# Output layer of an attention and gated-linear kernel: casts one tile ahead, subtractions moved from behind each pass's last product, an earlier split at the change of layers, one zero product instead of three

## The chip, the cores and the metric

One core of one Trainium2 chip. The metric is the device time of one execution in microseconds, as the median of several runs.

## The reference

Sigmoid attention over 8 batches and 12 heads (448 positions, head size 64), then a gated linear layer on the 3584 x 768 result, in fp32:

```python
scores = scale * np.matmul(q, k.transpose(0, 1, 3, 2)) - np.log(S)
attn = 1.0 / (1.0 + np.exp(-scores))
x = np.matmul(attn, v)            # heads side by side: (3584, 768)
gate = 1.0 / (1.0 + np.exp(-(x @ w_gate)))   # w_gate, w_val: 768 x 1536
val = x @ w_val
out = gate * val @ w_out                     # w_out: 1536 x 768
```

`w_gate`, `w_val` and `w_out` arrive as 64-bit floats and are brought to fp32 on the chip.

## The kernel before, in words

The work has three stages on TensorE, one behind the other: attention, the gate and value layer (GLU), and the output layer. Batches are taken in four pairs (`NPAIR`). The two linear layers use a Strassen-like scheme: each 2 x 2 block product is made of seven products (`NP`), so that a stage runs over seven combined operand tiles (index `i`) for each pair. Each operand is split into a high part, rounded to fp32r by a cast, and a low part, the difference. `product` (L316) makes three matmuls for each block: low weight by high operand, high weight by low operand, high by high.

For each operand tile there are therefore two steps before TensorE can use it: the cast on ScalarE (`high`, L164) and the subtraction on VectorE (`low`, L167). Both work on a tile of 128 x 1344. The source comes from DRAM by a load on SP's queue: `load_x` (L157) for the GLU, `load_h` (L337) for the output layer. The next load takes the buffer of a source that was subtracted, and SP waits for that.

All instructions are written in the program's order; each engine runs its own in that order. `tick()` is called after each group and runs what is due by then: stores, weight loads, and the casts and subtractions of weight tiles (`fetch_w`, L359: cast ten ticks after the load, L354, and subtraction twelve ticks after it, L357).

**Attention.** 168 beats (24 head groups by 7 key groups). A beat makes one scores product (L203), one sigmoid on ScalarE (L206) and the values product (L219) of two beats before. Before the first beat three zero products (L272 to L276) run on a zeroed tile. In the last beats the first GLU operands are loaded, x0 is cast and subtracted, and x1 is cast (L303), before the pending values products; x1 is subtracted after them (L308).

**GLU.** Three passes over the weights by four pairs by seven tiles `i` by four products `q` of nine matmuls. Behind a product its reader runs: a copy or sigmoid on ScalarE, an add (L328) or product (L331) on VectorE. Behind the last tile (`i` = 6) the result blocks are combined by subtractions (L420), on GpSimd, in the last half of the last pair on VectorE, and stored as `hs` (L374). The last two tiles (`left` 2 and 1) also prepare the output layer: cast of h0 and h1 at `q` = 1 of the two tiles (L430), subtraction and the next load at `q` = 2 (L434).

**Output layer.** Four pairs by seven passes `i` by three products `o`, each of 18 matmuls: nine with the operand tile h[m], nine with h[m+1]. Here m grows by two for each pass. The readers are copies on ScalarE for `i` = 0 and 1 (L476, L479) and adds on VectorE (L328) for the others. Even tiles have three buffers for the split operand and two for the source, odd tiles two and two (L340, L346). The order behind a product is:

```python
tick()
if o < 2:
    high_h(m + 2 + o)
if o > 0:
    low_h(m + 1 + o)
    load_h(m + 5 + o)
```

So h[m+2] is cast after the first product and subtracted after the second, and h[m+3] is cast after the second product and subtracted after the third, the last one of the pass.

Of the kernel before, what the change touches and what calls it, by code (L numbers as in the profile page):

```python
# [30 lines left out]
def sigmoid_attention_glu_kernel(ctx: ExitStack, tc: tile.TileContext, qk, v, wg, wv, wo, out):  # L31
# [34 lines left out]
    def tick(flush=False):  # L66
        clock[0] += 1
        due = [e for e in later if e[0] <= clock[0] or flush and e[2]]
        later[:] = [e for e in later if e not in due]
        for _, fn, _ in due:  # L70
            fn()
# [97 lines left out]
    def high_x(n):  # L169
        if n < len(x_order):  # L170
            ops[n] = op_tile()
            high(ops[n], x_loaded[n])
# [7 lines left out]
    with tc.manual_schedule(), tc.tile_pool(name="att", bufs=2) as att, tc.tile_pool(name="sc", bufs=2, space=PSUM) as scp, \  # L180
# [88 lines left out]
        units.load()  # L269
        zeros = att.tile([P, 2, S], F32, tag="a", name="a", bufs=3)[:, 0]  # L270
        nc.vector.memset(zeros, 0.0)
        for _ in range(3):  # L272
            sc = scp.tile([P, 2, 512], F32, tag="sc", name="sc")
            for h in range(2):
                for u in range(2):
                    nc.tensor.matmul(sc[halves[u], h, :S], lhsT=zeros[halves[h], :HP], rhs=zeros[halves[h]], start=True, stop=True)  # L276
        beats, beat, done = B * NQ * 7, 0, 0
        for m in range(B * NQ):
            for g in range(7):
                pending.append((m, g, scores(m, g)))  # L280
                if len(pending) > LAG:
                    values(*pending.pop(0))
                if g == 0:
                    load_qk(m + 1)
                if g == LAG:
                    load_v(m + 1)
                if m == 0 and g in (1, LAG):
                    units.load()
                tick()
                beat += 1  # L290
                while done < N_FIRST and done * (beats - 12) < beat * N_FIRST:
                    next(weights)
                    done += 1
                finish_adds()
                if beat == beats - 8:
                    load_x(0)
                    load_x(1)
                if beat == beats - 4:
                    high_x(0)
                if beat == beats - 3:  # L300
                    low_x(0)
                if beat == beats - 1:
                    high_x(1)  # L303
        while pending:
            values(*pending.pop(0))
            finish_adds()
            tick()
        low_x(1)  # L308
        tick(flush=True)

    with tc.manual_schedule(), tc.tile_pool(name="mm", bufs=8, space=PSUM, reuse_waits="tile") as mm:
# [37 lines left out]
        def low_h(m):  # L349
            if m < len(o_order):  # L350
                low(h_ops[m], h_loaded.pop(m))
# [17 lines left out]
        with tc.tile_pool(name="ff", bufs=1, reuse_waits="tile") as ff:  # L369
            def unit(tag, n):  # L370
                return ff.tile([P, S], F32, tag=tag, name=tag, bufs=n)

            def store_h(p, i, j, h):
                nc.sync.dma_start(out=h_src[p][i][j // 3][:, j % 3], in_=h)  # L374

            n = 0
            done, groups, all_groups = 0, 0, 8 * NP * NQUAD
            for s in range(NPASS):
                for p in range(NPAIR):
                    st = [{} for _ in range(NQUAD)]  # L380
                    if s == NPASS - 1 and p == NPAIR - 2:
                        for _ in weights:
                            pass
                    for i in range(NP):
                        for q in range(NQUAD):
                            d, t, jl = st[q], q % 2, q // 2
                            j = s * JS + jl
                            gate = st[q - 1] if t else None
                            if i in (0, 2, 5):
                                d["acc"] = bank()  # L390
                            acc = d["acc"]
                            product(acc, [(W[i][:, q], ops[n], (cols(k), k)) for k in range(HC)], i)
                            if i == 0:
                                d["s1"] = unit("s1", 6)
                                nc.scalar.copy(d["s1"], acc)  # L395
                            elif i == 1:
                                d["11"] = unit("v11" if t else "g11", 4)
                                if t:
                                    mul(d["11"], acc, gate["11"])
                                    after(2, lambda p=p, j=j, h=d["11"]: store_h(p, 0, j, h))  # L400
                                else:
                                    nc.scalar.activation(d["11"], acc, AF.Sigmoid)
                            elif i in (2, 3):
                                k = "u2" if i == 2 else "u3"
                                d[k] = unit(k, 5)
                                add(d[k], acc, d["s1"])
                            else:
                                k, to = {4: ("s1", 1), 5: ("u3", 6), 6: ("u2", None)}[i]
                                add(d[k], acc, d[k])
                                if t:  # L410
                                    mul(d[k], d[k], gate[k])
                                    if to is not None:
                                        after(2, lambda p=p, to=to, j=j, h=d[k]: store_h(p, to, j, h))
                                else:
                                    nc.scalar.activation(d[k], d[k], AF.Sigmoid)  # L415
                                if t and i == 6:
                                    t1, t2, t3, t4 = (unit("t", 7) for _ in range(4))
                                    for o, a, b in ((t1, d["u2"], d["11"]), (t2, d["u3"], t1), (t3, d["u3"], d["u2"]), (t4, d["s1"], t2)):
                                        engine = nc.vector if jl == 1 and s == NPASS - 1 and p == NPAIR - 1 else nc.gpsimd
                                        engine.tensor_tensor(out=o, in0=a, in1=b, op=ALU.subtract)  # L420
                                    for dly, to, h in ((3, 5, t1), (4, 2, t2), (5, 3, t3), (6, 4, t4)):
                                        after(dly + 2 * jl, lambda p=p, to=to, j=j, h=h: store_h(p, to, j, h))
                            tick()
                            left = len(x_order) - n
                            if q == 1:
                                high_x(n + 2)
                                if left in (4, 3):
                                    load_h(4 - left)
                                if left in (2, 1):
                                    high_h(2 - left)  # L430
                            if q == 2:
                                low_x(n + 2)
                                if left in (2, 1):
                                    low_h(2 - left)  # L434
                                    load_h(4 - left)
                            if q == 3:
                                if p == NPAIR - 1:
                                    nextW[i] = new_w(i)
                                    fetch_w(nextW[i], w_src[s + 1][i] if s + 1 < NPASS else o_src[i][:, :NQUAD])
                                if 0 <= 2 * NP - 2 - left < NP:  # L440
                                    fetch_wx(2 * NP - 2 - left)
                            if p < NPAIR - 1 and (s < NPASS - 1 or p < NPAIR - 2):
                                groups += 1
                                while done < N_REST and done * all_groups < groups * N_REST:
                                    next(weights, None)
                                    done += 1
                        ops.pop(n)
                        n += 1
                    if p == NPAIR - 1:
                        old, W[:] = list(W), [nextW[i] for i in range(NP)]  # L450
        with tc.tile_pool(name="fo", bufs=1, reuse_waits="tile") as fo:
# [1 line left out]
                return fo.tile([P, S], F32, tag=tag, name=tag, bufs=3)  # L453

            tick(flush=True)
            for m in range(4, 6):
                load_h(m)
            m = 0
            for p in range(NPAIR):
                st = [{} for _ in range(HC)]  # L460

# [4 lines left out]
                for i in range(NP):  # L466
                    for o in range(HC):
# [25 lines left out]
                                    save(o + mo, b, d[k], queue, a)  # L493
                        tick()
                        if o < 2:
                            high_h(m + 2 + o)
                        if o > 0:
                            low_h(m + 1 + o)
                            load_h(m + 5 + o)
                    h_ops.pop(m)  # L500
                    h_ops.pop(m + 1)
                    m += 2
# [36 lines left out]
```

## Time and profile before

| what | value |
|---|---|
| median of 3 runs | 1207.56 us (1204.35 to 1208.07) |
| profiled execution: its own time | 1207.19 us |
| its span, first to last instruction | 1205.4 us |
| TensorE matmul, busy | 1193.2 us, 99% |
| TensorE weight load, busy | 955.6 us, 79% |
| VectorE, ScalarE, GpSimd, busy | 722.3, 491.5, 321.7 us |
| attention, GLU, output layer (span) | to about 260, to about 883, to the end |

The profile lists instructions by engine: PE is the matmul, PEld the weight load that runs beside it, DVE VectorE, ACT ScalarE, POOL GpSimd, SP the queue that issues the DMAs. A matmul's recorded duration includes its way through the array, so matmuls overlap in the record and a busy PE can still lose time between them. In the timeline the square bracket names the idle time before an instruction and what ended it.

### The profile page before, as it was taken

How to read it: one execution, taken by the hardware profiler on the slowest of the kernel's cores; microseconds unless marked ns; L12 is line 12 of the kernel's file. 1: busy time of each engine (PE TensorE's matmuls, PEld its weight loads, DVE VectorE, ACT ScalarE, POOL GpSimd, SP SyncE). 2: the span in 40 equal slices, each digit the busy share in tenths (PEclk: the TensorE clock that was granted, in tenths of full speed). 3: DMA queues.
4: the chain of work that ended last, by engine and by line, in shares of the span. 5: the costliest groups of instructions: out<-in, count | busy, mean ns of one | idle time of the engine just before them, and what ended most of it. 6: DMA issues, size and time to landing. Idle time of an engine off the chain costs nothing.

```text
span 1205.4 us, 18247 instructions
## 1 busy us (share of the span) xinstructions
PE 1193.2 (99%) x7248; PEld 955.6 (79%) x7248; DVE 722.3 (60%) x827; ACT 491.5 (41%) x553; POOL 321.7 (27%) x244
## 2 busy tenths in 40 slices
PE   9999999999999999999999999999999999999998
PEld 3444444459999999899999999999988898898987
DVE  3344334437888858988876898747675424334333
ACT  6777777762322336232232623224344132132230
POOL 2161524251605315163450516414020000000000
PEclk9999999999999999999999999999999999999999
DMA  7585877877867777776758767466784543544441
GB/s 290 195 291 208 279 230 240 304 234 243 272 224 254 251 250 252 234 277 224 242 195 314 244 231 257 136 227 210 261 286 147 178 168 138 180 141 162 161 144 61
DMA packets 103077, 266.23 MB, mean 221 GB/s; under 512 B 10448, under 2 KB 74192, under 8 KB 102992
## 3 DMA queue, kind: packets, MB, share of 16 engines
q1 hardware_dynamic: 102848, 264.95, 64.1%
q8 instruction: 57, 0.93, 0.3%
q14 instruction: 28, 0.23, 0.1%
q10 hardware_dynamic: 144, 0.11, 0.0%
HBM read 176.95 MB, written 88.08 MB: 220 GB/s over the span
## 4 chain that ended last, share of the span: by engine, by line
PE 72%; DVE 4%; issue 1%; ACT 1%; DVEq 0%
PE acc L322 72%; DVE op L167 3%; DVE w L357 0%; ACT w L354 0%; DVE u L328 0%; ACT op L164 0%; DVE wsum L357 0%; DVE s L328 0%; PE av L219 0%; ACT wsum L354 0%; DVE s L331 0%; DVE u L331 0%; DVEq L534 0%; DVEq L328 0%; ACT u L415 0%
## 5 line engine op out<-in xcount | busy, mean ns | idle before, releaser
L322 PE MATMUL acc<-op,w 128*128 128x448 f32 x4032 | 845.3, 367 | 6.0 <-DVE op L167 4.1
L322 PEld LDWEIGHTS acc<-op,w 128*128 128x128 f32 x4032 | 755.8, 188 | 82.4 <-DVE op L167 12.0
L167 DVE TENSOR_TENSOR op<-src,op 128x1344 fp32r<-128x1344 f32 x140 | 233.3, 1666 | 70.8 <-ACT op L164 70.6
L164 ACT CAST op<-src 128x1344 fp32r<-128x1344 f32 x140 | 183.5, 1316 | 210.7 <-PE acc L322 139.9
L206 ACT ACTIVATE a<-sc,bias 128x896 f32<-128x896 f32 x168 | 169.0, 1007 | 66.5 <-PE sc L203 63.1
L203 PE MATMUL sc<-qk 64*64 64x448 f32 x1344 | 157.0, 538 | 0.4 <-ACT a L206 0.4
L219 PE MATMUL av<-a,v 64*64 64x448 f32 x1344 | 156.4, 536 | 0.7 <-ACT a L206 0.7
L328 DVE TENSOR_TENSOR u<-acc,s 128x448 f32<-128x448 f32 x120 | 74.2, 623 | 103.7 <-PE acc L322 103.3
L328 DVE TENSOR_TENSOR u<-acc,u 128x448 f32<-128x448 f32 (+1 forms) x121 | 73.8, 617 | 68.7 <-PE acc L322 68.6
L203 PEld LDWEIGHTS sc<-qk 64*64 64x64 f32 x1344 | 51.6, 134 | 76.5 <-issue 63.6
L219 PEld LDWEIGHTS av<-a,v 64*64 64x64 f32 x1344 | 51.4, 133 | 75.8 <-issue 74.0
L420 POOL TENSOR_TENSOR t<-u,v 128x448 f32<-128x448 f32 x23 | 37.9, 1648 | 224.9 <-DVE u L331 207.1
L129 POOL TENSOR_TENSOR wsum<-wf 128x384 f32<-128x384 f32 x18 | 20.7, 1153 | 231.7 <-DVE wf L117 231.7
L415 ACT ACTIVATE u<-u 128x448 f32<-128x448 f32 x48 | 27.8, 578 | 119.0 <-DVE u L328 115.0
L415 ACT ACTIVATE s<-s 128x448 f32<-128x448 f32 x24 | 13.9, 579 | 119.2 <-DVE s L328 119.1
L328 DVE TENSOR_TENSOR s<-acc,s 128x448 f32<-128x448 f32 x60 | 37.2, 622 | 40.4 <-PE acc L322 40.4
L322 PE MATMUL acc<-op,wr 128*128 128x448 f32 x216 | 50.7, 371 | 0.0
L245 DVE TENSOR_TENSOR op<-av,op 128x448 f32<-128x448 f32 x24 | 15.0, 623 | 58.9 <-ACT op L236 58.9
L395 ACT COPY s<-acc 128x448 f32<-128x448 f32 x48 | 25.5, 532 | 47.3 <-PE acc L322 41.5
L322 PEld LDWEIGHTS acc<-op,wr 128*128 128x128 f32 x216 | 41.4, 192 | 3.4
L245 DVE TENSOR_TENSOR x<-av,x 128x448 f32<-128x448 f32 x24 | 15.0, 624 | 48.1 <-ACT x L236 48.1
L420 POOL TENSOR_TENSOR t<-u,u 128x448 f32<-128x448 f32 x23 | 43.0, 1868 | 0.0
(51 smaller groups left out, 747.2 us busy)
## 6 DMA issues: line engine op xcount, KB each, us to landing
src<-xs SPq DMA_DIRECT2D x84, 672.0 KB, 4.7
src<-hs SPq DMA_DIRECT2D x56, 672.0 KB, 3.9
hs<-t SPq DMA_DIRECT2D x96, 224.0 KB, 5.2
qk<-qk SPq DMA_DIRECT2D x23, 896.0 KB, 5.0
v<-vv SPq DMA_DIRECT2D x24, 448.0 KB, 4.7
xs<-t SPq DMA_DIRECT2D x48, 224.0 KB, 4.1
w<-ws SPq DMA_DIRECT2D x14, 768.0 KB, 7.2
wr<-wg SPq DMA_DIRECT2D x12, 768.0 KB, 6.4
```

The lines of the kernel that those rows point to most:

```text
L129: nc.gpsimd.tensor_tensor(out=s1, in0=a21, in1=a22, op=ALU.add)
L164: nc.scalar.copy(op[:, 0], src)
L167: nc.vector.tensor_tensor(out=op[:, 1], in0=src, in1=op[:, 0].bitcast(F32), op=ALU.subtract)
L203: nc.tensor.matmul(sc[halves[u], h, :S], lhsT=qkt[halves[h], p, k0:k0 + HP], rhs=qkt[halves[h], p, :S], start=True, stop=True)
L206: nc.scalar.activation(a, sc[:, :, :S], AF.Sigmoid, bias=bias, scale=scale)
L219: nc.tensor.matmul(avs[key][halves[h], :S], lhsT=vt[halves[u], g, h], rhs=a[halves[u], h], start=start, stop=g == last)
L245: nc.vector.tensor_tensor(out=x, in0=other, in1=x, op=ALU.add)
L322: nc.tensor.matmul(acc, lhsT=a, rhs=b, start=first and n == 0, stop=n == len(terms) - 1, skip_group_check=not first)
L328: nc.vector.tensor_tensor(out=o, in0=a, in1=b, op=ALU.add)
L395: nc.scalar.copy(d["s1"], acc)
L415: nc.scalar.activation(d[k], d[k], AF.Sigmoid)
L420: engine.tensor_tensor(out=o, in0=a, in1=b, op=ALU.subtract)
```

## The change

There are four edits. One zero product is made instead of three. The cast of x1 moves behind the pending values products. In the last GLU tile, h1 is cast after group 0 and subtracted after group 1 (before: 1 and 2); h0 stays where it was. In the output layer, h5 is loaded before h4, h2 is cast before the first product, and behind the products the order is: after the first, subtract h[m+2], load h[m+6], cast h[m+3]; after the second, subtract h[m+3], load h[m+7]; after the third, cast h[m+4].

```diff
-        for _ in range(3):
-            sc = scp.tile([P, 2, 512], F32, tag="sc", name="sc")
-            for h in range(2):
-                for u in range(2):
-                    nc.tensor.matmul(sc[halves[u], h, :S], lhsT=zeros[halves[h], :HP], rhs=zeros[halves[h]], start=True, stop=True)
+        sc = scp.tile([P, 2, 512], F32, tag="sc", name="sc")
+        for h in range(2):
+            for u in range(2):
+                nc.tensor.matmul(sc[halves[u], h, :S], lhsT=zeros[halves[h], :HP], rhs=zeros[halves[h]], start=True, stop=True)
...
-                if beat == beats - 1:
-                    high_x(1)
         while pending:
             values(*pending.pop(0))
             finish_adds()
             tick()
+        high_x(1)
         low_x(1)
...
-                                if left in (2, 1):
-                                    high_h(2 - left)
                             if q == 2:
                                 low_x(n + 2)
-                                if left in (2, 1):
-                                    low_h(2 - left)
-                                    load_h(4 - left)
+                            if (left, q) in ((2, 1), (1, 0)):
+                                high_h(2 - left)
+                            if (left, q) in ((2, 2), (1, 1)):
+                                low_h(2 - left)
+                                load_h(4 - left)
...
-            for m in range(4, 6):
+            for m in (5, 4):
                 load_h(m)
             m = 0
+            high_h(2)
...
                         if o < 2:
-                            high_h(m + 2 + o)
-                        if o > 0:
-                            low_h(m + 1 + o)
-                            load_h(m + 5 + o)
+                            low_h(m + 2 + o)
+                            load_h(m + 6 + o)
+                        if o != 1:
+                            high_h(m + 3 + o // 2)
```

## Rows read from the trace of the kernel before

**Rows 1.** The page, busy us, share of the span and instructions of each engine.

```profile
PE 1193.2 (99%) x7248; PEld 955.6 (79%) x7248; DVE 722.3 (60%) x827; ACT 491.5 (41%) x553; POOL 321.7 (27%) x244
```

**Rows 2.** Timeline, output layer, one pass: start, duration, engine, line, tiles.

```profile
1040.77 0.62 DVE L328 TENSOR_TENSOR u<-acc,u 128x448 f32<-128x448 f32 x1 [3.03 <-PE acc L322]
...
1044.42 0.63 DVE L328 TENSOR_TENSOR u<-acc,u 128x448 f32<-128x448 f32 x1 [1.56 <-PE acc L322]
1044.96 1.55 DVE L167 TENSOR_TENSOR op<-src,op 128x1344 fp32r<-128x1344 f32 x1
...
1046.56 0.30 PEld L322 LDWEIGHTS acc<-op,w 128*128 128x128 f32 x2 [0.53 <-DVE op L167]
```

**Rows 3.** Waits of PEld, 895 to 1205: us in total, times, longest.

```profile
PEld acc L322 <- DVE op L167: 10.2, 20, 0.5
```

**Rows 4.** Timeline, last readers of the output layer's first and last pass.

```profile
898.15 0.53 ACT L476 COPY s<-acc 128x448 f32<-128x448 f32 x1 [1.89 <-PE acc L322]
...
1201.85 0.69 DVE L328 TENSOR_TENSOR u<-acc,u 128x224 f32<-128x224 f32 x2 [3.02 <-PE acc L322]
```

**Rows 5.** The page, DMA issues: count, size, median us to landing.

```profile
src<-hs SPq DMA_DIRECT2D x56, 672.0 KB, 3.9
```

**Rows 6.** Timeline, change from the GLU to the output layer.

```profile
882.70 1.46 ACT L354 CAST w<-w 128x1536 fp32r<-128x1536 f32 x1
...
884.07 1.30 ACT L164 CAST op<-src 128x1344 fp32r<-128x1344 f32 x1
...
885.40 1.91 DVE L167 TENSOR_TENSOR op<-src,op 128x1344 fp32r<-128x1344 f32 x1 [1.42 <-ACT op L164]
...
885.42 0.47 PE L322 MATMUL acc<-op,w 128*128 128x448 f32 x1 [1.05 <-ACT op L164]
...
887.37 0.91 PE L322 MATMUL acc<-op,w 128*128 128x448 f32 x2 [1.48 <-DVE op L167]
...
892.48 0.63 DVE L420 TENSOR_TENSOR t<-s,t 128x448 f32<-128x448 f32 x1 [1.01 <-DMA hs<-t]
...
894.69 1.56 DVE L167 TENSOR_TENSOR op<-src,op 128x1344 fp32r<-128x1344 f32 x1
```

**Rows 7.** Busy time by stretch behind the change; the tenth column is the granted clock.

```profile
888.00:889.00 1.00, 1.00 (x4) 0.87 (x4) 0.90 (x2) 0.00 (x0) 1.00 (x2) 0.50 0.83 204
```

**Rows 8.** Timeline, end of attention.

```profile
257.51 1.32 ACT L164 CAST op<-src 128x1344 fp32r<-128x1344 f32 x1
...
258.72 1.02 ACT L206 ACTIVATE a<-sc,bias 128x896 f32<-128x896 f32 x1
...
259.79 0.98 PE L219 MATMUL av<-a,v 64*64 64x448 f32 x8 [0.72 <-ACT a L206]
...
261.96 2.24 DVE L167 TENSOR_TENSOR op<-src,op 128x1344 fp32r<-128x1344 f32 x1
```

**Rows 9.** Timeline, start of the kernel.

```profile
1.42 4.76 PE L276 MATMUL sc<-a 64*64 64x448 f32 x24 [1.42 <-DVE a L271]
2.12 0.43 SPq L194 DMA_DIRECT2D v<-vv  x1
...
5.95 2.20 PE L203 MATMUL sc<-qk 64*64 64x448 f32 x16
...
7.48 1.90 ACT L206 ACTIVATE a<-sc,bias 128x896 f32<-128x896 f32 x2 [5.25 <-PE sc L203]
...
8.53 0.98 PE L203 MATMUL sc<-qk 64*64 64x448 f32 x8 [0.39 <-ACT a L206]
```

**Rows 10.** Instructions of L276 and L203: ns min/median/max, first and last start.

```profile
L276 PE MATMUL sc<-a x24: 951/951/1004, 1.4 to 5.2; 64*64 64x448 f32 x24
...
L203 PE MATMUL sc<-qk x1344: 535/536/951, 6.0 to 257.0; 64*64 64x448 f32 x192
L203 PEldq EVENT_SEMAPHORE  x25: 51/51/51, 3.6 to 245.4; - x25
```

**Rows 11.** DMA issues between 2.1 and 2.6 us: count, size, us to landing.

```profile
v<-vv SPq DMA_DIRECT2D x1, 448.0 KB, 5.4
```

## The prediction

> **What bounds the kernel now.** The page comes first: TensorE is busy for 99% of the span [rows 1], so only what makes TensorE wait, or run slower, is worth anything, and whatever ScalarE, VectorE and the queues gain on the side is worth nothing. Next comes the timeline of one tile of the output layer [rows 2]. One pass of `i` is three products of 18 matmuls; the accumulator readers L328 stand 3.65 us apart (1040.77 to 1044.42), so a matmul costs 0.203 us and a pass without a wait 10.95 us. Behind the last product VectorE runs first the add of that product (1044.42) and then the subtraction of the second operand tile (1044.96, 1.55 us), and the weight load for that tile is released only at 1046.56 after 0.53 us of idle. This is a wait by program order: the subtraction stands behind an add that waits for the product's end, while TensorE has only ten matmuls of the next pass (2.03 us) before it needs the result. The waits of the stage say how often: 20 times for this subtraction [rows 3]. What it is worth is read from the two ends of the layer [rows 4]: from the last reader of pass 0 (898.15) to the last reader of pass 27 (1201.85) are 303.70 us, and 27 passes at 10.95 are 295.65, so 8.05 us are lost there.
>
> The other places are found in the timeline of the three seams: the start, the last beats of attention, and the change of layers. The profiled execution took 1207.19 us, 0.37 below the median of 1207.56; I make the sum against it.
>
> **The output layer.** After the change the cast of the next tile's first half stands behind the third product of the pass before, that of its second half behind the first product, and the subtractions stand behind the first and second products. From the start of a pass, VectorE then does: add at 3.65 (0.62), subtraction 4.2 to 5.75, add at 7.3, subtraction 7.85 to 9.4, add at 10.95. TensorE needs the two results at 10.95 and 12.98, so both are early by over 1.5 us. In passes with ScalarE readers there are no adds, and the order is looser. Nothing is added: the same casts, subtractions, loads and stores. What could be late next is a load. SP issues a load right behind the subtraction that frees its buffer, now one product earlier than before, and the y stores that share SP keep their places; a load lands in 3.9 us [rows 5] and is cast about two passes later, so two passes hide it. Taken: 8.05, all of it. Bounds: 7.0 (a wait left in the first passes, where the weight subtractions L357 also run) and 8.05.
>
> **The change of layers.** In before, TensorE runs nine matmuls of the output layer, then needs the second half, h1: its cast ends at 885.37, its subtraction runs 885.40 to 887.31, and TensorE resumes at 885.42 for one matmul and at 887.37 for good [rows 6]. The cast stood behind a weight cast L354 (882.70, 1.46 us). Moved one group up, it takes that place: 882.70 to 884.02. The subtraction then takes 884.05 to 885.96 if it lasts 1.91 us as here, beside GpSimd's four subtractions, or to 885.60 at the 1.55 of [rows 2]; I take 1.91, the row of the same place. TensorE resumes at 886.0 and not 887.37: 1.35 us. The weight cast, one sigmoid and the add behind them move back by about a cast; their readers are passes away or off TensorE's path. The load of h3, which SP issues behind this subtraction, and all the `hs` stores behind it move up by the same 1.35.
>
> A second term hangs on this. After the stall the granted clock was 0.50, the lower of the two levels, 1.2 GHz [rows 7]. Its price: from 887.37 to the end of pass 0 are 44 matmuls, 8.92 us at full rate plus 0.16 of the last one's tail, so the reader at 898.15 should have stood at 896.45: 1.70 us. TensorE idled here twice, 1.05 and 1.48 us with one matmul between. After the change it is one idle of about 1.6. The only nearer row is the idle of 0.72 at the end of attention, after which matmuls went on at full pace [rows 8]. The value is 1.70 if the clock holds and 0 if it falls again; I take 1.70, since there is less than two thirds of the idle time and it is in one piece. With it the layer change is worth 3.05, with bounds 1.35 and 3.4.
>
> Pass 1 must not be held in turn: its second matmul wants the subtraction of h2 at 886.0 + 44 x 0.203 + 0.2 = 895.15. In before this ran 894.69 to 896.25 behind the last `t` subtraction on VectorE (892.48), which waits for an `hs` store to land [rows 6]. That store is 1.35 earlier, so the subtraction ends about 894.9. If it does not move, pass 1 waits 1.1 us; this stays as a bound.
>
> **The end of attention.** ScalarE casts x1 from 257.51 and only then runs the last sigmoid at 258.72; TensorE waits 0.72 us and starts its last products at 259.79 [rows 8]. With the cast behind the pending products, the sigmoid begins when ScalarE is free, about 257.6, and ends at 258.6, before TensorE's products in hand end (259.79 less 0.72, 259.07; full pace would have started the next at 258.89). Gain 0.9. The cover for what moves: the cast follows the last accumulator copy, ends by 262.4, and its subtraction, 2.24 us in before, by 264.7; x1 is needed after four groups of nine matmuls, 7.3 us from the layer's start near 259.8, so at 267.1. The load of x3 behind it on SP slips by some 0.5 us and is not read for two passes. Bounds 0 and 1.0.
>
> **The start.** The three zero products hold TensorE from 1.42 to 5.95 [rows 9], each matmul 951 ns against 536 later [rows 10]: the lower level, which the column of granted clock does not show here. The first scores could start at 3.7, since the wait on their data ended at 3.6 [rows 10]. With one zero product TensorE is free at 2.9, so scores run 3.7 to 5.2 and 5.2 to 6.7 at the slow pace. The first sigmoid comes at 5.25 and not 7.48, and the third scores at 6.7 and not 8.53. The first v, needed about 7.6, lands at 2.12 + 5.4 = 7.5 [rows 9, 11]. In before the pace rose near 7.0, between the last slow scores and the sigmoid at 7.48 that followed. If it rises at the same time, the start gains 1.83 - 0.15 = 1.7. If the gap before 3.7 makes TensorE begin anew, and it takes as long as from 1.42 to 7.0, it rises at 9.3 and 2.3 us at half pace take back 1.15: 0.55. I take the middle, 1.1; the ends are -0.3 (a rise at 11) and 1.7.
>
> The Trainium skill speaks against this part: "TensorE: Matmul & The Clock Gate", section "Part 1: The HAM clock gate (the "warmup" mystery)", says that the slow level is the default and that sustained activity releases it, so that warm-up is a matter of busy time, and matmuls on zeros are not wasted while they provide it. By that rule the start would give 0.55 or less, by the row's time of rise 1.7. The trace agrees so far as the zero products ran slow and the scores after them rose.
>
> **Sum.** 8.05 + 3.05 + 0.9 + 1.1 = 13.1, so 1207.2 - 13.1 = 1194.1 us.
>
> **Rivals.**
> The clock falls at the layer change all the same (1.6 us idle is enough): the sum loses 1.70, 1195.8. For it: a single known fall, after 2.5 us. Chance 0.25.
> The pace rises late at the start: the term is -0.3 and not 1.1, 1195.5. For it: 0.8 us of idle that was not there. Against it: from 3.7 on TensorE is as busy as before. Chance 0.15. That is what the Trainium skill's section named above would make likely.
> The change does not do what it says: TensorE's wait in the output layer is for the subtraction's own inputs and stays; 1207.2 - 5.05 = 1202.1. Against it: the subtraction starts 0.54 us after the add, while its cast, 1.3 us, was done earlier in the pass. Chance 0.05.
> All gains are off the path or eaten, within 0.3%: chance 0.03.
> Slower: the pace stays at the lower level through the first beats of attention because the zero products no longer carry TensorE to the data. Each microsecond there costs half of one, so it decides against the change from (13.1 + 3.6) / 0.5 = 33 us on, that is past 40 us; at 45 us it gives 1207.2 - 13.1 + 19 = 1213. Against it: scores and values run back to back from 8.53 on. Chance 0.02.
>
> **How the numbers follow.** A difference below 0.3%, 3.6 us, cannot be told from none, as the runs of before spread over 3.7. The forecast has 0.50. Faster: 0.50 + 0.25 + 0.15 + 0.05 = 0.95; same 0.03; slower 0.02. The range: all gains at their upper bounds give 8.05 + 3.4 + 1.0 + 1.7 = 14.2, 1193.0, and the runs of before reach 3.2 below their median, of which I give 2.5: 1190.5. At the other end both clock rivals together and 1 us held in pass 1 give 1194.1 + 1.7 + 1.4 + 1.1 = 1198.3; I take 1198.5.
>
> **What would show it.** Right: no wait of weight loads for the subtraction L167 behind 895; readers of the last product 10.95 apart; the first third-score product at 6.7; the last values without idle; at the layer change one idle of 1.6 us and the clock at 1.00 behind it. Wrong: waits of some 0.5 us left per pass, new waits of TensorE for ScalarE's casts, or granted clock of 0.50 in more places than one.

## The result, and the profile after

The changed kernel took 1194.48 us as the median of 6 runs (1190.90 to 1198.70), the kernel before 1207.26 (1204.30 to 1208.35, 6 runs). The medians differ by 12.78 us; the ratio taken over the single runs is 0.9906 with a 95% interval of 0.9879 to 0.9932: faster by 0.9%. The forecast was 1194.1. The profiled execution took 1194.63 us with a span of 1192.9; against the profile before that is 12.5 us less of span.

The waits of TensorE in the whole profile after, first of the matmuls, then of the weight loads behind the change of layers (us in total, times, longest):

```profile
PE acc L320 <- DVE op L167: 1.6, 1, 1.6
PE sc L275 <- DVE a L271: 1.4, 1, 1.4
PE acc L320 <- DVE u L326: 0.7, 1, 0.7
PE av L219 <- DMA v<-vv: 0.7, 1, 0.7
PE sc L203 <- DMA qk<-qk: 0.3, 1, 0.3
```

```profile
PEld acc L320 <- DVE op L167: 1.9, 1, 1.9
```

Where [rows 3] had 20 waits for the subtraction from 895 on, the second list, taken from 880 on, has one, and that is the idle at the change of layers. The timeline of one pass after (start, duration, engine, line, tiles, idle before):

```profile
1017.87 0.62 DVE L326 TENSOR_TENSOR u<-acc,u 128x448 f32<-128x448 f32 x1 [3.02 <-PE acc L320]
...
1018.41 1.55 DVE L167 TENSOR_TENSOR op<-src,op 128x1344 fp32r<-128x1344 f32 x1
...
1019.99 0.33 SPq L339 DMA_DIRECT2D src<-hs  x1
...
1021.52 0.62 DVE L326 TENSOR_TENSOR u<-acc,u 128x448 f32<-128x448 f32 x1 [1.56 <-PE acc L320]
...
1022.06 1.55 DVE L167 TENSOR_TENSOR op<-src,op 128x1344 fp32r<-128x1344 f32 x1
...
1025.17 2.54 ACT L164 CAST op<-src 128x1344 fp32r<-128x1344 f32 x2 [8.41 <-PE acc L320]
1025.17 0.62 DVE L326 TENSOR_TENSOR u<-acc,u 128x448 f32<-128x448 f32 x1 [1.56 <-PE acc L320]
...
1028.82 0.62 DVE L326 TENSOR_TENSOR u<-acc,u 128x448 f32<-128x448 f32 x1 [3.02 <-PE acc L320]
...
1189.33 0.69 DVE L326 TENSOR_TENSOR u<-acc,u 128x224 f32<-128x224 f32 x2 [3.02 <-PE acc L320]
```

Behind the last product (1025.17) VectorE now has the add alone; the next product's reader follows 3.65 us later, as within a pass. The two subtractions are done by 1023.6. The casts run ahead of them, two in a row (1025.17). The last row answers to [rows 4]: the last reader stands at 1189.33.

The change of layers after, the counterpart of [rows 6], and its granted clock (tenth column), that of [rows 7]:

```profile
881.16 1.30 ACT L164 CAST op<-src 128x1344 fp32r<-128x1344 f32 x1
...
882.36 1.47 ACT L352 CAST w<-w 128x1536 fp32r<-128x1536 f32 x1
882.49 2.07 DVE L167 TENSOR_TENSOR op<-src,op 128x1344 fp32r<-128x1344 f32 x1 [0.58 <-ACT op L164]
...
884.62 0.67 PE L320 MATMUL acc<-op,w 128*128 128x448 f32 x2 [1.57 <-DVE op L167]
...
893.84 0.53 ACT L475 COPY s<-acc 128x448 f32<-128x448 f32 x1 [3.02 <-PE acc L320]
```

```profile
885.00:888.00 3.00, 3.00 (x17) 2.78 (x16) 2.72 (x4) 2.81 (x4) 3.00 (x3) 1.00 0.80 234
```

Cast and weight cast have changed places, TensorE idles once, 1.57 us, and the granted clock stays at 1.00, the 2.4 GHz level.

The two seams of attention after, for [rows 8] and [rows 9], and the place where VectorE gave some of it back:

```profile
3.51 4.09 PE L203 MATMUL sc<-qk 64*64 64x448 f32 x24 [0.32 <-DMA qk<-qk]
...
5.35 1.01 ACT L206 ACTIVATE a<-sc,bias 128x896 f32<-128x896 f32 x1 [3.12 <-PE sc L203]
...
8.27 0.98 PE L219 MATMUL av<-a,v 64*64 64x448 f32 x8 [0.66 <-DMA v<-vv]
...
227.37 0.57 DVE L111 TENSOR_SCALAR wf<-wr 128x768 uint32<-128x768 uint32 x1 [6.82 <-DMA ws<-wf]
...
229.04 0.62 DVE L245 TENSOR_TENSOR op<-av,op 128x448 f32<-128x448 f32 x1
...
257.10 1.01 ACT L206 ACTIVATE a<-sc,bias 128x896 f32<-128x896 f32 x1
...
259.18 6.14 PE L320 MATMUL acc<-op,w 128*128 128x448 f32 x29
259.22 0.53 ACT L236 COPY x<-av 128x448 f32<-128x448 f32 x1 [1.11 <-PE av L219]
259.65 1.32 ACT L164 CAST op<-src 128x1344 fp32r<-128x1344 f32 x1
```

The last sigmoid starts with ScalarE free, no values product waits for it, and the cast of x1 follows the last accumulator copy. At 227.37 VectorE stands for 6.8 us before L111, which writes a `wf` buffer whose store has not landed; the add L245 behind it, which frees an accumulator, runs late.

Step by step, on the marks that both profiles share (us from the span's start):

| mark | before | after | gained there |
|---|---|---|---|
| first accumulator copy of attention, L236 | 15.06 | 14.04 | 1.02 |
| third-last accumulator copy of attention | 251.08 | 250.49 | -0.43 |
| first GLU matmul | 260.70 | 259.18 | 0.93 |
| TensorE resumes at the change of layers | 887.37 | 884.62 | 1.23 |
| last reader of pass 0 | 898.15 | 893.84 | 1.56 |
| last reader of pass 27 | 1201.85 | 1189.33 | 8.21 |

### The profile page after: what moved, and what is told of

The parts are those of the page before. It is cut to its first block, busy times and chain, and to the rows that moved or that the text cites. A ratio compares the mean times of both kernels' runs of the same rounds, so it can differ in the third digit from the quotient of the medians.

```text
span 1192.9 us, 18213 instructions
## 1 busy us (share of the span) xinstructions
PE 1184.6 (99%) x7232; PEld 960.1 (80%) x7232; DVE 721.8 (61%) x827; ACT 490.4 (41%) x553; POOL 321.7 (27%) x244
## 4 chain that ended last, share of the span: by engine, by line
PE 96%; DVE 2%; DMA 1%; ACT 1%; issue 0%; SPq 0%; DVEq 0%
PE acc L320 75%; PE av L219 11%; PE sc L203 10%; DVE op L167 1%; DMA v<-vv 1%; DMA hs<-v 0%; DVE w L355 0%; ACT w L352 0%; ACT op L164 0%; DVE u L326 0%; DVE wsum L355 0%; DVE v L329 0%; SPq L189 0%; DVE s L326 0%; ACT wsum L352 0%
## 5 line engine op out<-in xcount | busy, mean ns | idle before, releaser
L203 PE MATMUL sc<-qk 64*64 64x448 f32 x1344 | 165.5, 542 | 0.3 <-DMA qk<-qk 0.3
L219 PE MATMUL av<-a,v 64*64 64x448 f32 x1344 | 164.3, 536 | 0.7 <-DMA v<-vv 0.7
L203 PEld LDWEIGHTS sc<-qk 64*64 64x64 f32 x1344 | 55.0, 134 | 74.9 <-issue 60.0
L219 PEld LDWEIGHTS av<-a,v 64*64 64x64 f32 x1344 | 55.4, 133 | 73.5 <-issue 70.5
L245 DVE TENSOR_TENSOR op<-av,op 128x448 f32<-128x448 f32 x24 | 14.9, 623 | 57.4 <-ACT op L236 57.4
L245 DVE TENSOR_TENSOR x<-av,x 128x448 f32<-128x448 f32 x24 | 15.0, 624 | 46.7 <-ACT x L236 46.7
L117 DVE SCALAR_TENSOR_TENSOR wf<-wr,wf 128x768 uint32<-128x768 uint32 x36 | 42.5, 1181 | 0.3
```

The source lines that it names most:

```text
L117: nc.vector.scalar_tensor_tensor(out=a, in0=raw[:, :, 0], scalar=29, in1=a, op0=ALU.logical_shift_right, op1=ALU.bitwise_or)
L203: nc.tensor.matmul(sc[halves[u], h, :S], lhsT=qkt[halves[h], p, k0:k0 + HP], rhs=qkt[halves[h], p, :S], start=True, stop=True)
L219: nc.tensor.matmul(avs[key][halves[h], :S], lhsT=vt[halves[u], g, h], rhs=a[halves[u], h], start=start, stop=g == last)
L245: nc.vector.tensor_tensor(out=x, in0=other, in1=x, op=ALU.add)
```

## The experiments

Unless a median is named, each kernel was run once, with a profile. The kernel before, run beside them, took 1207.51 us (old order, casts in one pass, split late and split sooner), 1211.10 (the first four tests on the seams of attention) and 1206.94 as the median of 11 runs (the others). Single times of one and the same kernel spread by some 10 us, for a reason that the runs themselves brought out, so a verdict rests on a stretch of the profile and not on the total. The reason comes first, as the other readings need it.

**Two paces of TensorE.** The changed kernel once more, unedited:

> The changed kernel once more, unedited. Theory, TensorE takes one of two paces (203 or 207 ns a matmul) when it resumes from an idle: median 1190 to 1199 us, single runs some 4 us apart, in a profile no wait in the output layer, and the difference to the profile read first explained by stretches at the other pace. Rival, the time of the changed kernel is fixed but for noise: all runs within 1.5 us of 1194.5.

Its 6 runs gave 1191.98 us as median and went from 1188.33 to 1195.20; the kernel before, 11 runs beside it, 1206.94, from 1200.92 to 1208.53. The ratio over the runs is 0.9887 (0.9860 to 0.9913). So the time is not fixed but for noise. What differs shows in stretches of 140 us each in which TensorE never waits: the number of matmuls in them (second column behind the bounds, in brackets). First the profile after that was read above, then the kernel with three zero products, then that with both casts in one pass:

```profile
300.00:440.00 140.00, 140.00 (x692) 129.73 (x691) 111.15 (x129) 45.08 (x55) 54.68 (x36) 1.00 0.76 256
520.00:660.00 140.00, 140.00 (x679) 127.17 (x678) 109.12 (x127) 43.66 (x52) 52.73 (x34) 1.00 0.74 251
700.00:840.00 140.00, 140.00 (x679) 127.17 (x678) 103.47 (x121) 45.00 (x58) 55.99 (x36) 1.00 0.62 208
910.00:1050.00 140.00, 140.00 (x693) 129.76 (x692) 60.02 (x58) 35.15 (x34) 0.00 (x0) 1.00 0.47 163
```

```profile
520.00:660.00 140.00, 140.00 (x693) 129.76 (x692) 111.83 (x130) 44.38 (x54) 53.34 (x35) 1.00 0.75 257
700.00:840.00 140.00, 140.00 (x693) 129.72 (x692) 105.47 (x122) 48.42 (x61) 55.77 (x36) 1.00 0.66 218
```

```profile
300.00:440.00 140.00, 140.00 (x680) 127.15 (x679) 110.74 (x129) 45.23 (x55) 54.80 (x36) 1.00 0.74 249
...
910.00:1050.00 140.00, 140.00 (x679) 127.16 (x678) 58.62 (x57) 37.29 (x34) 0.00 (x0) 1.00 0.48 165
```

There are two counts, 692 or 693 and 679 or 680, and nothing between, at a granted clock of 1.00 in both: 203 and 207 ns a matmul by the readers (a product of 18 takes 3.65 or 3.72 us). The tests ran on three chips, and both paces occur on each, so it is not the chip. The pace holds until the matmuls or only the weight loads have waited for something, near 490 and near 692 in the GLU and at the change of layers, and can be the other one afterwards; in the profile of this unedited run it went from 207 to 203 ns where weight loads had been idle for 0.20 and 0.30 us. The GLU has 3024 matmuls and the output layer 1512, so at 4 ns each the two can differ by 12 and 6 us from run to run. The profiles before and after happen to have the same paces in the same stretches (203 ns up to the wait near 490, 207 from there to the change of layers, 203 in the output layer), which is why the table above adds up without a correction. In the tests, a stretch is compared between kernels with the same paces.

**The old order of the output layer** in the changed kernel:

```diff
-            for m in (5, 4):
+            for m in range(4, 6):
                 load_h(m)
             m = 0
-            high_h(2)
...
                         if o < 2:
-                            low_h(m + 2 + o)
-                            load_h(m + 6 + o)
-                        if o != 1:
-                            high_h(m + 3 + o // 2)
+                            high_h(m + 2 + o)
+                        if o > 0:
+                            low_h(m + 1 + o)
+                            load_h(m + 5 + o)
```

> The changed kernel with the old order of the output layer (casts and subtractions behind the products as before, h4 loaded ahead of h5). Theory, program order on VectorE: the subtraction of h[m+3] stands again behind the add of the last product, so some 17 to 20 waits of about 0.5 us of weight loads for it come back, and the stretch from the last reader of pass 0 to the last reader of pass 27 goes from 295.5 us back to 303.5 to 304: total about 1202.5. Rival, the time came from elsewhere (the earlier split, or the clock that held): the stretch stays below 298 and the total below 1197.

Measured: 1198.83 us in one run, and in its profile, from 880 on,

```profile
PEld acc L320 <- DVE op L167: 10.1, 20, 0.5
```

The waits are back to their number, and the stretch from the last reader of pass 0 (889.25) to that of pass 27 (1193.53) is 304.28 us, against 295.49 after. The theory holds for the stretch; the total came out 3.7 us below it, because this execution had the 203 ns pace in all of the GLU: from the first GLU matmul to the last reader of pass 0 it took 629.76 us, against 634.66 after.

**The new order alone**, in the kernel before (the same edit the other way round):

> The kernel before with the new order of the output layer alone (three zero products, the early cast of x1 and the later split stay). Theory: from the last reader of pass 0 to the last reader no wait of weight loads for the subtraction is left, and the stretch is one of the two paces without a wait, 27 x 10.95 = 295.5 us or 27 x 11.16 = 301.3 us; the change of layers idles 2.5 us as before. Rival, the new order needs the earlier split to get ahead: waits of about 0.5 us remain in the passes of the first pair at least.

Measured: 1204.46 us. The change of layers idles 1.05 and 1.48 us as before, and the granted clock falls behind it. No wait for the subtraction is left behind pass 0, and the stretch is 1199.15 - 897.83 = 301.32 us: 27 passes of 11.16, the other pace, without a wait. (The slower pace does not hide the wait: the ten matmuls that cover the subtraction last 0.04 us longer at it, and the wait was 0.5.) The part does its work without the earlier split, the rival is out.

**Is it the casts one tile ahead?** Both casts behind the first product of the same pass, subtractions as changed:

```diff
             m = 0
-            high_h(2)
...
+                        if o == 0:
+                            high_h(m + 2)
+                            high_h(m + 3)
                         if o < 2:
                             low_h(m + 2 + o)
                             load_h(m + 6 + o)
-                        if o != 1:
-                            high_h(m + 3 + o // 2)
```

> The changed kernel with both casts of the next tile behind the first product of the pass, none ahead across passes, and the subtractions where the change put them (behind the first and second product). Theory: only the place of the subtraction counts, since a cast of 1.3 us is ready long before; stretch of the output layer 295.5 us, no weight-load wait for the subtraction but the one at the change of layers, total 1194 to 1195. Rival, the casts one tile ahead are what removes the wait: waits of 0.5 us per pass come back, total 1199 to 1203.

Measured: 1204.71 us, which by the total alone would have been read as the rival's case. The profile says otherwise. The weight loads wait for the subtraction once from 880 on, at the change of layers as in the changed kernel (1.9 us), and the stretch of the output layer is 1199.41 - 898.11 = 301.30 us, 27 passes of 11.16 without a wait. This execution had the 207 ns pace throughout, in the GLU and in the output layer. So the place of the subtraction removes the wait; casts a whole tile ahead are not needed for it.

**The split at the change of layers, as late as before:**

```diff
-                            if (left, q) in ((2, 1), (1, 0)):
+                            if (left, q) in ((2, 1), (1, 1)):
                                 high_h(2 - left)
-                            if (left, q) in ((2, 2), (1, 1)):
+                            if (left, q) in ((2, 2), (1, 2)):
```

> The changed kernel with h1 cast and subtracted one group later again, as before the change. Theory: at the change of layers TensorE idles 2.5 us in two pieces and not 1.6, 1.2 us more, and the granted clock falls to 0.50 behind it, another 1.6: the reader of the last product of pass 0 about 2.8 us later, total about 1197.4. Rival, the clock's fall in before had another cause: 1.2 us later only, granted clock 1.00, total 1195.8.

Measured: 1198.94 us. TensorE waits as in [rows 6], 1.03 and 1.48 us, but the clock stays up; timeline, then stretches:

```profile
880.98 0.47 PE L320 MATMUL acc<-op,w 128*128 128x448 f32 x1 [1.03 <-ACT op L164]
882.92 0.68 PE L320 MATMUL acc<-op,w 128*128 128x448 f32 x2 [1.48 <-DVE op L167]
```

```profile
884.00:886.00 2.00, 2.00 (x12) 1.81 (x11) 1.86 (x3) 1.12 (x2) 1.38 (x1) 1.00 0.80 247
```

The kernel with the early cast of x1 (below) had the same paces up to the change of layers and the changed split: from the first GLU matmul to the last reader of pass 0 it took 631.38 us, this one 632.72. Of the 1.34 more, 44 matmuls at 4 ns are 0.18, so the later split costs 1.16 us. The clock's fall is not tied to it. The other half of this test came unasked: the kernel with the old order of the output layer has the changed split and idled 0.18 and 1.62 us, and there the clock fell; that with three zero products idled 0.20 and 1.62, and there it did not. First the one, then the other:

```profile
880.00:883.00 3.00, 3.00 (x10) 2.69 (x9) 2.86 (x3) 2.07 (x3) 2.00 (x2) 0.50 0.89 314
```

```profile
880.00:883.00 3.00, 3.00 (x16) 2.79 (x15) 2.80 (x3) 3.00 (x4) 2.44 (x2) 1.00 0.90 304
```

Both had the 203 ns pace in most of the GLU: 629.76 and 628.29 us from the first GLU matmul to the last reader of pass 0, so the fall to 0.50 costs 1.5 us. Whether it comes is not settled by the length of the idle. Whether it matters that the idle is in one piece stays open: in all five profiles with a single idle of 1.57 to 1.59 us at the change of layers (after, its repetition, both casts in one pass, early cast of x1, v first) the clock held, and of the six with the idle in two pieces it fell in three.

**The split sooner still**, h1 cast behind the last group of the tile before and subtracted behind group 0:

```diff
-                            if (left, q) in ((2, 1), (1, 0)):
-                                high_h(2 - left)
-                            if (left, q) in ((2, 2), (1, 1)):
+                            if (left, q) in ((2, 1), (2, 3)):
+                                high_h(q // 3)
+                            if (left, q) in ((2, 2), (1, 0)):
```

> The changed kernel with h1 cast still two groups sooner (behind the last group of the tile before) and subtracted one group sooner. Theory: the cast no longer waits for the sigmoid behind VectorE's weight subtraction, the subtraction ends about 882.2 on this clock of before 884.6, ahead of TensorE, and the idle of 1.57 us at the change of layers is gone: total about 1193.0. Rival, VectorE's adds that now stand behind it hold TensorE instead, or pass 1 waits for h2: a new wait of TensorE there, total 1194.5 or above.

Measured: 1194.77 us. The idle at the change of layers is gone: the subtraction of h1 ran from 880.87 to 882.42 and nothing waited. But pass 1 then waits, as the rival had it:

```profile
892.18 3.01 DVE L167 TENSOR_TENSOR op<-src,op 128x1344 fp32r<-128x1344 f32 x2
...
893.78 1.49 PE L320 MATMUL acc<-op,w 128*128 128x448 f32 x6 [1.11 <-DVE op L167]
```

The subtraction of h2 stands on VectorE behind the last adds, four GLU subtractions and a weight subtraction, and TensorE, which is early now, meets it. The unedited repetition had the same paces up to there: against it the stretch from the first GLU matmul to the last reader of pass 0 is 1.66 us shorter (633.24 against 634.90), and that to the last reader of pass 27 only 0.27 (930.12 against 930.39). With **h2 cast and subtracted ahead of those four subtractions** as well:

```diff
                                     t1, t2, t3, t4 = (unit("t", 7) for _ in range(4))
+                                    if n == len(x_order) - 1 and jl == 1:
+                                        high_h(2)
+                                        low_h(2)
...
             m = 0
-            high_h(2)
...
                         if o < 2:
-                            low_h(m + 2 + o)
+                            if m + o > 0:
+                                low_h(m + 2 + o)
```

> The kernel with h1 split two groups sooner, and h2 cast and subtracted ahead of the last four subtractions of the GLU on VectorE. Theory: the idle at the change of layers (1.6 us) stays away and pass 1 no longer waits 1.1 us for h2, so TensorE has no wait over 0.3 us from 690 us on; from the first GLU matmul to the last reader of pass 0 at the pace of the changed kernel 1.5 to 1.6 us less. Rival: the four subtractions and the weight subtraction behind h2 come too late instead, and TensorE waits for h3 or for a weight tile.

Measured: 1191.35 us. From the first GLU matmul to the last reader of pass 0 629.73 us, 1.65 less than the 631.38 at the same paces up to there, as the theory had it; but then h3 is late by 0.72 us, and to the last reader of pass 27 the gain is 926.24 against 926.87, only 0.6 us. Theory and rival were both half right: VectorE has more work queued at this seam than there is time for, and in these two tests what was moved ahead made the next thing late.

**The seams of attention.** The early cast of x1 restored:

```diff
                     low_x(0)
+                if beat == beats - 1:
+                    high_x(1)
         while pending:
             values(*pending.pop(0))
             finish_adds()
             tick()
-        high_x(1)
```

> The changed kernel with the cast of x1 ahead of the last sigmoid again. Theory: the last values product waits 0.7 us for the sigmoid and the first GLU matmul stands 0.9 us later against the last beats; total about 1195.4. Rival: the sigmoid is late anyway, behind the accumulator copy, and the wait is below 0.3 us.

Measured: 1192.59 us. The last values product waits 0.71 us for the sigmoid, and from the third-last accumulator copy of attention to the first GLU matmul are 9.62 us (250.80 to 260.42) against 8.69 after: 0.93, the theory's number.

Three zero products restored:

```diff
-        sc = scp.tile([P, 2, 512], F32, tag="sc", name="sc")
+        for _ in range(3):
+            sc = scp.tile([P, 2, 512], F32, tag="sc", name="sc")
...
```

> The changed kernel with three zero products again. Theory: the first values product starts at 9.3 and not 8.3 us, and steady beats stand 1.0 us later; total about 1195.5. Rival, the zero products had kept the pace up and nothing was gained at the start: steady beats within 0.3 us of those of the changed kernel.

Measured: 1188.92 us. The first values product starts at 9.40 and the first accumulator copy stands at 15.12, 1.08 later than after. At the end of attention, though, the first GLU matmul is at 259.81, only 0.63 later than after (259.18), and the other executions with one zero product, the late cast of x1 and v in its old place lie between 259.26 and 259.89. Averages over the profiles say it better. With three zero products (three profiles) the first accumulator copy stands at 14.95 and the third-last at 250.98; with one, and v in its old place (eight profiles), at 14.22 and 250.83. So 0.73 us is gained at the start and 0.15 is left by the end of attention. That is less than the third-last copy varies between executions of one kind (250.70 to 251.15 with three, 250.49 to 251.20 with one; the profile after is the earliest). With three zero products VectorE never makes TensorE wait near 229; with one or none TensorE's weight loads wait there 0.3 to 0.8 us for the add L245.

No zero product at all:

```diff
-        zeros = att.tile([P, 2, S], F32, tag="a", name="a", bufs=3)[:, 0]
-        nc.vector.memset(zeros, 0.0)
-        sc = scp.tile([P, 2, 512], F32, tag="sc", name="sc")
...
```

> The changed kernel with no zero product. Theory A, the data sets the start and the pace rises by time or by the scores alone: scores start at 3.5 as with one zero product and the steady beats stand within 0.4 us. Theory B, work on zeros counts toward the rise of the pace: scores stay at 951 ns longer, and steady beats come up to 1.0 us later. In neither does anything change after the start.

Measured: 1189.89 us. The data landed a little later in this execution, the scores started at 3.77 and took 4.00 us for 24 matmuls, against 3.51 and 4.09 after. The first copy stands at 14.36; in the executions with one zero product it stands between 14.04 and 14.44. Theory A, as far as one execution shows: work on zeros bought nothing. Nor does the rise of the pace follow the zero products: the last matmul of 0.9 us or more starts at 5.22 to 5.97 with three of them (three profiles), at 4.47 to 9.11 with one (ten profiles), and at 6.08 here.

v loaded ahead of the third part of q and k:

```diff
                 for p, lo, hi in parts:
+                    if m == 0 and p == 1:
+                        load_v(0)
                     nc.sync.dma_start(out=loads[m][0][:, p, lo:hi], in_=qk[m // NQ, m % NQ][:, p, lo:hi])
...
         load_qk(0)
-        load_v(0)
         units.load()
```

> The changed kernel with the first load of v issued ahead of the third part of the first load of q and k. In the changed kernel the first values product waits 0.66 us for that load. Theory: v lands about 1 us sooner, the wait goes, and the steady beats stand 0.6 us earlier: total about 1193.9. Rival: the fourth scores product then waits for the third part of q and k, or the sigmoid of the first beat is the next wait, and nothing is gained.

Measured: 1200.32 us, with the 207 ns pace in two thirds of the GLU and in the output layer. The first values product starts at 7.36 and no longer waits, the first copy stands at 13.24, 0.80 sooner than after. Near 229 the weight loads then wait 0.7 us for the add L245, and the first GLU matmul is at 258.83, 0.35 sooner. Right at the start, half given back.

**All the gains together**: h2 ahead, v first, and the stores of split weights one tick sooner:

```diff
-                    after(4, store)
+                    after(3, store)
```

> As the kernel with h1 split two groups sooner and h2 ahead of the last subtractions, and with v loaded ahead of the third part of q and k and the stores of split weights one tick sooner. Theory: 1.6 us at the change of layers, 0.9 at the start, and of that the 0.4 to 0.7 not given back near 229 us where VectorE waited for such a store: 2.5 us below the changed kernel at the same pace, so about 1192 us; the two paces of TensorE spread the runs by some 4 us on either side. Rival: the stores hold SP's queue sooner, loads behind them come late, and nothing is gained.

Measured: 1191.96 us as the median of 6 runs (1188.57 to 1193.69), ratio to the kernel before 0.9891 (0.9865 to 0.9916), and the changed kernel beside it 1191.98. No difference in the total. In its profile v was not waited for, but the pace rose late, and the first values product still ran slow (1.69 us against 0.98 after):

```profile
3.81 4.76 PE L205 MATMUL sc<-qk 64*64 64x448 f32 x24 [0.61 <-DMA qk<-qk]
8.34 1.69 PE L221 MATMUL av<-a,v 64*64 64x448 f32 x8
```

The first GLU matmul stands at 260.08, later than after. The earlier stores did not remove the wait near 229: weight loads wait 0.4 us there. Nothing waits at the change of layers, but pass 1 does, for 1.46 us at 889.42. This execution had the 203 ns pace in the whole of the GLU and the output layer, as those with three and with no zero product had. From the first GLU matmul to the last reader of pass 0 it took 625.90 us, against 628.29 and 628.23; to the last reader of pass 27 923.10, against 923.77 and 923.71. So 2.4 us were gained at the seam and 0.6 kept, as with h2 ahead.

## Why the prediction was right

**The output layer** was forecast at 8.05 and gave 8.21. That the wait came from program order on VectorE is shown from both sides, by the old order put back and by the new order alone. The cover named for what moves held: no load made TensorE wait in the output layer, and the passes of the first pair had no wait.

**The change of layers**, stall: forecast 1.35, measured 1.23. The cast did take the weight cast's place, and the subtraction started with it, but lasted 2.07 us and not the 1.91 taken; GpSimd's subtractions ran beside it in both. The test with the late split gives 1.16.

**The clock behind it**: forecast 1.70, measured 1.56, but the reason given for it is not shown. The step said that the clock would hold "since there is less than two thirds of the idle time and it is in one piece". The first half failed: the clock held after the old idle of 2.5 us in one kernel and fell after it in two others, it fell after one of 1.8, and with idles equal to 0.02 us it did either. The second half agrees with all five profiles that have the idle in one piece, but nothing tests it. With the 203 ns pace in all of the GLU the changed split idles in two pieces (0.2 and 1.62 us), and of three such profiles one had the fall; so the term is in part luck, and in single runs the rival with the clock falling can hold.

**The end of attention**: forecast 0.9, measured 0.93, and undone alone 0.93.

**The start**: forecast 1.1, measured 1.02, and for another reason than those weighed, so the close number is luck. The middle was taken between two times at which the pace might rise. In the profile after it rose near 7 as in before, and the third scores product started at 6.55, near the 6.7 that was named; by that case 1.7 would have been gained. What took 0.66 of it was v, which landed at 2.12 + 6.1 and not at 2.12 + 5.4. In other executions the pace rose later (the last slow matmul starts at 8.35 with h2 ahead and at 9.11 with all the gains), so the rival with the late rise occurs too. The Trainium skill's section that was weighed against this part ("TensorE: Matmul & The Clock Gate", "Part 1: The HAM clock gate (the "warmup" mystery)") says that the slow level is the default and that activity releases it. The traces agree that the slow pace comes first: the first matmuls take 951 ns in the profiles before and after, and 536 later. That work on zeros counts was the prediction's own inference, and no run here shows a use of it: without any zero product the first copy stood at 14.36, within the spread of 14.04 to 14.44.

**What was missed.** In the profile after 0.43 of the start's gain is given back near 229: VectorE waits for a store to land, and an add that TensorE needs stands behind that. The working looked for what is late at the seams and not for a wait tied to a transfer in the middle of attention, which does not move along when TensorE gets ahead. The 0.59 left there is the best draw of eight; on the averages the two zero products removed were worth 0.15 us by the end of attention.

In sum 13.1 was forecast and 12.5 measured, about 0.4 of it by that draw. The two sets of 6 runs of the changed kernel have medians of 1194.48 and 1191.98, both inside the range of 1190.5 to 1198.5, but single runs went from 1188.33 to 1198.70: the spread that was taken from three runs of before (3.7 us) was too narrow, since the two paces were not known.

## What to carry to other kernels

Where the work for the next tile stands behind the reader of this tile's last product on an in-order engine, the slack is what the tensor engine can still do without it; put it behind an earlier reader, and the order alone is worth most of the waits (here 8.2 of the 10.2 us that the weight loads waited). A stage that gets ahead meets the next thing tied to a transfer or to another engine's backlog, so follow a gain to the end of its stage before counting it. And compare stretches between marks, with the pace of the work in each: totals of a single execution would have turned several of these experiments the wrong way.

## What the runs showed of the hardware that was not expected

TensorE runs the same stream of matmuls, without a wait and at a granted clock of 1.00, at one of two paces 2% apart (some 692 or 679 matmuls in 140 us), keeps it for hundreds of microseconds, and can change it where matmuls or weight loads have waited. What chooses between them was not found. The resumption at the change of layers on the end of a VectorE subtraction led to either.

The granted clock fell to 0.50 for some 3 us behind some idles at the change of layers and not behind others of the same or greater length (fell: 2.5 us in before and in before with the new order alone, 1.8 with the old order; held: 1.57 after and 1.57 to 1.59 in four more, 1.8 with three and with no zero product, 2.5 with the late split). A fall costs 1.5 us.

At the start the matmuls take 951 ns for some microseconds before they take 536, and the moment of the rise differs between executions (last slow matmul at 4.47 to 9.11 us with one zero product). With v loaded first, the first accumulator copy stood at 13.24 with the early rise and at 14.84 with the late one.
